# A gated delta-rule attention with a spatial MLP on one core: k's products of the first group as 64x64 tiles, a shorter norm, a new order of operations

## The chip, the cores and the metric

The kernel runs on one core of one Trainium2 chip. The metric is device time in microseconds (us) of one launch. PE is TensorE, DVE is VectorE, ACT is ScalarE, POOL is GpSimd, and SP issues the DMAs. Lower is better.

## The reference, cut to what matters

The input has 4 batches, 8 heads, 768 positions and 48 channels. The attention is a recurrence over positions, and its output feeds a gated MLP with a spatial mixing matrix.

```python
k_n = k / (np.linalg.norm(k, axis=-1, keepdims=True) + 1e-06)
for t in range(S):
    y[:, :, t] = einsum('bhd,bhde->bhe', q[:, :, t], state)
    v_old = einsum('bhde,bhd->bhe', state, k_n[:, :, t])
    state = state + beta_t * einsum('bhd,bhe->bhde', k_n[:, :, t], v[:, :, t] - v_old)
x = y as (batch, 768, 384)
h = np.maximum(x @ w_in, 0.0);  u, v = h[..., :512], h[..., 512:]
v_n = (v - mean(v)) / sqrt(var(v) + 1e-6)
gated = u * (einsum('ts,bsd->btd', w_spatial, v_n) + b_spatial[None, :, None])
out = gated @ w_out
```

## The kernel before, in words

The recurrence is done in chunks of 64 positions. There are 24 steps; a step is one chunk of 2 of the 4 batches, for all heads (16 chains at once), so steps 0 to 11 are one pair of batches and 12 to 23 the other. Four steps form a group, and there are six groups.

For each group, `prep` makes the small triangular matrices that a chunk needs. PE multiplies each chunk of k with itself (`kk`), ACT or DVE copies the products from PSUM to a buffer xt (helper L392), and DVE transposes the diagonal blocks so that each chain sits on a lane of its own (`la`, L576). From the diagonal of the products the norm of k follows (L584 to L591), with it the lane data are scaled (L594 or L598), and the triangular systems are solved on the lanes by forward substitution. Groups 0 and 1 (mode "w") do that on DVE in 16 columns (`lanes16`, L630 to L636, 29 instructions) and are widened to 32 by more matmuls (`widen16`, L706 on); groups 2 to 5 (mode "p") do it on POOL in 32 columns (`lanes`, L615 and L620, 61 instructions). L645 transposes the result back into xt, and `widen` brings each step from 32 to 64 columns.

A step then runs in a fixed chain: `a` on PE (k times the state), DVE subtracts it from v (L782), `b` on PE, ACT copies it (w, L810), `c` on PE, and DVE adds it to the state (S, L823, or L825 in step 0). `qs` and `pu` on PE give the output y, which ACT copies to xs (L841). Two steps make 128 positions of x, which six small DMAs put in order (L858); ACT and DVE split x into a high and a low part (xh L862, xl L863), and then the MLP of these positions can start on PE (`mlp_v`, `mlp_u`; later `mlp_g` and `mlp_o`). A step's chunk of k or q is 256 KB. The weight w_in comes as 64-bit floats in six pieces of 512 KB and is turned into a high and a low part by ten instructions for each piece (L455 to L471) on ACT, DVE and POOL.

Every operation is first added to a plan. `ORDER` is a list written out by hand, two letters for each operation, in which the operations are issued; each engine takes its own in that order and none overtakes another. A pair of letters past the last operation is a filler: a matmul of the mask `mpos` with itself into a free bank, whose result nobody reads. `PICK` chooses the engine where an operation may run on two. The names with L are lines of the profile.

Of the kernel before, what the change touches and what calls it, by code (L numbers as in the profile page):

```python
# [11 lines left out]
ALU = mybir.AluOpType  # L12
# [21 lines left out]
FULL = False  # L34
# [5 lines left out]
    "0407090605000102030J0Y080A0B0KQW0@0*0[QW0D0]0^0_0E0C0L0+0G0|0-0.0/0F0H0I0;1N0<1OQW1Y0N2U0M1P0P2R0:2S2V21221C2XQW2a0Q"  # L40
    "0{1Q0R1R0S0T0U0V1T0W0XQW0}0Z0b0c0d0e0f0g0a0h0i0j0k0l0m0n0oQW0p0q0r0s0tQW112T0u2Y0vQW0wQW0x5K240yQW2W1S0z2Z0O0!QW0#1D"
    "2b375N0$5W3G2c1U5L5Q1k1Z0%2f0~0,QW0&5O2d5T25125MQW38QW0(36100=0>1V1W270?28292D2e1l2h2A2E1E1F1G1I1a2g1H5P2B2C3Q2F132,"
    "3031322N3R0)1K2I2i33142k1m1b2m1c1e1n15171o2t341f2l1dQW162H2G2J3J3S2K1r5R1h2M3539QW2n1q2o2p2q2r2s3F1g19182O5S2j3K3A2u"
    "3L1p5U5V1J3M233H3N8R262P3B1A5Z3O451B3P1i1L1t1X1M2w2x2L2yQW2z2!2#2$3C2%3T2&3~2v2Q2(2)3U2*2+QW2-2.3D5X5Y5a3V3W3X3,403E"
    "QW3a413Y2/2:2;2<2=2>5b4L3Z463b42435c5d4447482?QW4A5e5f5g5h5i5j2@492[2]2^2_4M4N3I8U3eQW4O3i4B3kQW4CQW3h8d3j3d3l3c3f3g"
    "4P4QF74H4S4D4T4FQW5l2{5k5n2|1s5o5p5q2}3m4E4V4R4U4X4W4Y4G4Z4a4c5r8S5s8V2~8T5t515u5v5w8W5x4d5y525z1u1j5!4I3n4b504J1v4m"
    "536U3.3/3:4l5#3o565$4k4f4n4j4i4K4e8a5%8X5&1w1x556V5(5)5*5+5-575.5/3u1y5:1z5;5<5=3v3p5B3q5859546M5A3w5C3;3<6N3=6O5>5D"
    "6T5?3?1!6P3@6Q6R3r6W3[3s3]3^1#3t5@5[5]5^5_5F6j6S5m6X1%5E5{5G5|6k5}6l1$1&3x3y3z3>4o5~1(4h5,3_6Y6f6g1)6m6Z7O4p6a606d6n"
    "61623{6b8Y6c8Z5H6e5I3!5J6o3}1*QW3#631+647W8b7P8c7Q8e4q4g6q7X7R4:4]6566676p1-7S6r68694^4;6t6$4_4<3$1.3%3|8h3&7T6A6s6B"
    "1:6C6D6E6F6G6u7l7U6v6w6&6h6%3(6x1;8f8g4=4{6y4>6!6#6i6)6+6.6-6*6/7m7n1/4r7o4s6H6I6z8i7Y7t7p7h7q1=6J6K7s7V3)8j7r4?4t7u"  # L50
    "7Z6L8l8m4w4|4x7a7b4y7i7j6(8k3*8n8o6:8p8q6;7c7f7d8s4z4!7g9T7e8r9U4u4#4v7v7&8u4}7x4~8v8w8x8y7w7y78798z4@4,9V9q7)7(7A8!"
# [31 lines left out]
PICK = (
    "00000111111100110111011100110010000000100000000000000011001100001100010000000000000000000010010011010010000010000000"
    "00000000000000001000000000100110000010101110100110000000001010010000000000010100101110011011001000000110110100011010"
    "11111100011000100000100010100110100100"
# [181 lines left out]
def delta_rule_gated_mlp(  # L268
# [23 lines left out]
    cst = new("cst", 3)  # L292
# [74 lines left out]
    gd = new("gd", 32)  # L367
# [158 lines left out]
    def prep(g):  # L526
# [56 lines left out]
        bl = bl_[g % 2]  # L583
        P.add("ACT", 0.35, lambda: nc.scalar.activation(out=sq, in_=dg, func=AF.Sqrt, bias=cst[:, 1:2]), rd=[kla, "cst"], wr=["sq"], pr=p0)  # L584
        P.add("ACT", 0.32, lambda: nc.scalar.activation(out=gd, in_=sq, func=AF.Identity, scale=0.5, bias=cst[:, 2:3]), rd=["sq", "cst"], wr=["gd"], pr=p0)
        P.add("DVE", 0.35, lambda: nc.vector.reciprocal(out=t0_, in_=sq), rd=["sq"], wr=["t0"], pr=p0, port=True)
        P.add("DVE", 0.18, lambda: nc.vector.tensor_mul(out=t0_, in0=t0_, in1=dg), rd=[kla], wr=["t0"], pr=p0, port=True)
        P.add("DVE", 0.18, lambda: nc.vector.scalar_tensor_tensor(out=n_l, in0=t0_, scalar=0.5, in1=gd, op0=ALU.mult, op1=ALU.add), rd=["t0", "gd"], wr=["nl"], pr=p0, port=True)
        P.add("DVE", 0.18, lambda: nc.vector.tensor_mul(out=t0_, in0=n_l, in1=n_l), rd=["nl"], wr=["t0"], pr=p0, port=True)
        P.add("DVE", 0.35, lambda: nc.vector.reciprocal(out=t0_, in_=t0_), wr=["t0"], pr=p0, port=True)  # L590
        P.add("DVE", 0.18, lambda: nc.vector.tensor_mul(out=dv, in0=t0_, in1=bl), rd=["t0", ("bl", g % 2)], wr=["sq"], pr=p0, port=True)  # L591
        if mode == "w":
# [530 lines left out]
```

## Time and profile before

| | |
|---|---|
| median of 3 runs | 472.31 us (469.68 to 477.03) |
| the profiled execution: own time | 471.3 us |
| its span, first to last instruction | 469.6 us |
| mean granted TensorE clock | 0.941 of full speed |
| PE busy, matmuls | 427.7 us, 91% of the span |
| DVE, ACT, POOL busy | 248.5, 230.6, 236.4 us |

The time outside the span is 1.7 us. Busy time of PE is the union of matmuls that overlap, so a busy PE is not always PE at its peak. A granted clock of 1.00 is the upper of two levels (2.4 GHz), one of 0.50 the lower (1.2 GHz), and a value between them is a stretch that holds both.

### The profile page before, as it was taken

The numbers are of one execution on the slowest core, as the hardware profiler recorded it, in microseconds if no ns is written. First come the engines' busy times: TensorE is split into PE (matmuls) and PEld (weight loads), VectorE is DVE, ScalarE is ACT, GpSimd is POOL, SyncE is SP. The second block draws the span as 40 slices with busy tenths as digits, with TensorE's granted clock in tenths as the row PEclk, the third lists the DMA queues.
The fourth block names the chain that finished last, engine by engine and source line by source line (L and its number), as shares of the span: only waits on it lengthen the run. The fifth ranks groups of instructions, "written<-read, shape, count | busy, mean of one in ns | idle before, by whom it ended". The sixth has DMA issues, their size and how long they took to land.

```text
span 469.6 us, 21728 instructions
## 1 busy us (share of the span) xinstructions
PE 427.7 (91%) x9736; PEld 379.4 (81%) x9736; DVE 248.5 (53%) x558; ACT 230.6 (49%) x546; POOL 236.4 (50%) x371
## 2 busy tenths in 40 slices
PE   4865986988989999899899999999989999999997
PEld 3654764776777787689899999898888899999996
DVE  4899786375857773686335653425345142251221
ACT  4547634156656677885223553512555570451112
POOL 3274548883468980468973488884213300411220
PEclk9575599798999999899999999999999999999999
DMA  7660314411454455433251023123150000001002
GB/s 273 219 209 25 99 49 125 154 47 57 131 154 139 138 165 175 142 94 103 67 155 44 20 59 109 39 66 116 42 164 3 10 1 0 2 35 50 35 35 84
DMA packets 26109, 42.65 MB, mean 91 GB/s; under 512 B 4512, under 2 KB 14880, under 8 KB 26016
## 3 DMA queue, kind: packets, MB, share of 16 engines
q1 hardware_dynamic: 26016, 41.27, 28.4%
q8 instruction: 76, 1.25, 1.1%
q14 instruction: 17, 0.14, 0.1%
HBM read 35.36 MB, written 4.72 MB: 85 GB/s over the span
## 4 chain that ended last, share of the span: by engine, by line
PE 81%; issue 5%; DVE 3%; ACT 3%; DMA 3%; SPq 2%; POOL 2%; ACTq 0%; DVEq 0%; POOLq 0%
PE ps L524 81%; SPq L411 2%; DMA bn<-in_k_t 2%; ACT xt L392 1%; DMA bn<-in_bun 1%; POOL ut L470 1%; POOL ut L469 1%; ACT w L810 1%; DVE la L576 0%; DVE xt L645 0%; DVE ut L464 0%; DMA xs<-xs 0%; DVE g L464 0%; ACT xs L841 0%; DVE pt L757 0%
## 5 line engine op out<-in xcount | busy, mean ns | idle before, releaser
L524 PE MATMUL ps<-wsph,vf 128*128 128x256 f32 x528 | 107.2, 285 | 0.0
L524 PEld LDWEIGHTS ps<-wsph,vf 128*128 128x128 f32 x528 | 86.6, 190 | 1.1
L620 POOL TENSOR_TENSOR wl<-wl,prod 128x60 f32<-128x60 f32 (+7 forms) x120 | 76.4, 636 | 9.1
L615 POOL TENSOR_TENSOR prod<-wl,la 128x60 f32<-128x60 f32 (+7 forms) x120 | 70.4, 586 | 9.3
L524 PE MATMUL ps<-wspl,vf 128*128 128x256 f32 x264 | 74.6, 283 | 0.0
L524 PEld LDWEIGHTS ps<-wspl,vf 128*128 128x128 f32 x264 | 50.3, 191 | 0.3
L980 DVE TENSOR_TENSOR gt<-ps,bbc 128x512 f32<-128x512 f32 x24 | 16.5, 689 | 52.6 <-PE ps L524 52.5
L524 PE MATMUL ps<-wout_h,g 128*128 128x384 f32 x128 | 35.2, 339 | 0.0
L392 ACT COPY xt<-xt 32x128 f32<-32x128 f32 (+1 forms) x85 | 29.3, 345 | 5.4 <-DVE xt L392 3.6
L524 PE MATMUL ps<-bn 64*64 64x64 f32 (+2 forms) x896 | 19.7, 232 | 9.7 <-DMA bn<-in_k_t 5.9
L983 POOL TENSOR_TENSOR gt<-gt,ut 128x512 f32<-128x512 f32 x11 | 15.1, 1372 | 25.4 <-DVE gt L980 25.3
L524 PEld LDWEIGHTS ps<-bn 64*64 64x64 f32 (+1 forms) x896 | 16.2, 139 | 13.4 <-issue 10.3
L810 ACT COPY w<-ps 128x384 f32<-128x384 f32 x24 | 11.5, 481 | 29.8 <-PE ps L524 29.8
L524 PE MATMUL ps<-mpos 128*128 128x256 f32 x64 | 24.8, 508 | 1.2 <-ACT xs L841 1.0
L985 ACT CAST g<-gt 128x512 fp32r<-128x512 f32 x16 | 9.9, 621 | 31.8 <-DVE gt L983 20.4
L524 PE MATMUL ps<-ke 64*64 64x64 f32 (+2 forms) x768 | 18.4, 254 | 6.7 <-ACT wl L642 3.3
L985 ACT CAST xt<-gt 128x512 fp32r<-128x512 f32 x8 | 5.0, 620 | 39.5 <-POOL gt L983 22.9
L524 PEld LDWEIGHTS ps<-ke 64*64 64x64 f32 (+1 forms) x768 | 15.6, 158 | 10.2 <-issue 4.0
L524 PEld LDWEIGHTS ps<-wout_h,g 128*128 128x128 f32 x128 | 22.9, 188 | 0.3
L757 DVE TENSOR_TENSOR pt<-ps,mpos 128x512 f32<-128x512 f32 (+1 forms) x27 | 16.6, 625 | 11.6 <-PE ps L524 11.3
L887 ACT ACTIVATE vr<-ps 128x512 f32<-128x512 f32 x22 | 13.1, 595 | 18.5 <-PE ps L524 18.3
L739 POOL TENSOR_TENSOR bn<-bn,nn 128x384 f32<-128x384 f32 x14 | 11.9, 854 | 20.0 <-DVE ps L633 5.1
(206 smaller groups left out, 1068.2 us busy)
## 6 DMA issues: line engine op xcount, KB each, us to landing
bn<-in_bun SPq DMA_DIRECT2D x46, 256.0 KB, 3.1
bn<-in_bun SPq DMA_DIRECT2D x48, 192.0 KB, 3.4
ke<-in_k_t SPq DMA_DIRECT2D x22, 256.0 KB, 3.0
out<-ob SPq DMA_DIRECT2D x24, 192.0 KB, 2.0
vf<-in_w_in SPq DMA_DIRECT2D x6, 512.0 KB, 6.1
g<-in_w_sp SPq DMA_DIRECT2D x3, 768.0 KB, 5.3
g<-in_w_out SPq DMA_DIRECT2D x4, 384.0 KB, 4.2
xs<-xs SPq DMA_DIRECT2D x66, 16.0 KB, 2.5
```

The costliest lines, as they stand in the source:

```text
L392: (nc.scalar.copy if e == "ACT" else ENG[e].tensor_copy)(out=out_, in_=in_)
L411: return P.add("SP", 0.39 if k.get("kb") else 0.57, lambda: nc.sync.dma_start(out=out_() if callable(out_) else out_, in_=in_() if callabl ...
L524: nc.tensor.matmul(o, l, r, start=start, stop=stop)
L615: P.add("POOL", cost, lambda: nc.gpsimd.tensor_tensor(out=pt if j else dst, in0=w3[:, :n, j : j + 1].broadcast_to([128, n, m]), in1=la3[:, ...
L620: P.add("POOL", cost, lambda: nc.gpsimd.tensor_tensor(out=dst, in0=dst, in1=pt, op=ALU.add), rd=["prod"], wr=[kw], pr=p0 + 2)
L739: P.add("", {"DVE": 0.56, "POOL": 0.83}, fn=lambda e: ENG[e].tensor_tensor(out=v, in0=v, in1=n.unsqueeze(3).broadcast_to([128, 2, 4, HD]), ...
L757: nc.vector.tensor_tensor(out=pt.rearrange("p (d a c) -> p d a c", d=2, a=2)[:, d], in0=v.rearrange("p d (a c) -> p d a c", a=2), in1=mpos ...
L810: P.add("ACT", 0.48, lambda: nc.scalar.copy(out=v3(w, 192), in_=v3(pc, 512)[:, :, 0:192]), rd=["pc"], wr=[("w", s % 2)], pr=pr)
L887: P.add("ACT", 0.69, lambda: nc.scalar.activation(out=raw_(r), in_=bank(h.unit), func=AF.Relu, accum_out=st[:, j : j + 1]), rd=[("pv", i)] ...
L980: P.add("DVE", 0.69, lambda: nc.vector.tensor_tensor(out=gt(), in0=v3(bank(h.unit), 256), in1=bbc[0][:, th * 256 : th * 256 + 256].unsquee ...
L983: P.add("", both(512), fn=lambda e: ENG[e].tensor_mul(out=gt_[t.unit], in0=gt_[t.unit], in1=u_(uh)[:, half * 512 : half * 512 + 512]), rd= ...
L985: P.add("ACT", 0.6, lambda: nc.scalar.copy(out=gv(gg)[0][:, hs], in_=gt_[t.unit]), rd=[kk], wr=[("gh", b, th, half)], pr=q)
```

## The change

There are three parts. First, `FULL` makes `prep` of group 0 issue the same 16 products of 64x64 for each chunk as the other groups do (32 smaller ones before), and the four copies that put the lower blocks in place (`za`, 32 partitions by 512) now run for group 0 too. Second, the norm is worked out another way. Third, `ORDER` and `PICK` are new: 34 fillers before, one after, and 2376 operations in place of 2372.

```diff
-FULL = False
+FULL = True
-    cst = new("cst", 3)
+    cst = new("cst", 2)
-    gd = new("gd", 32)
+    gd, n2 = new("gd", 32), new("n2", 32)
-        for i, x in enumerate((0.0, 1e-30, EPS)):
+        for i, x in enumerate((0.0, 1e-36)):
-        ACT  sq = activation(dg, Sqrt, bias=1e-30)
-        ACT  gd = activation(sq, Identity, scale=0.5, bias=EPS)
-        DVE  t0 = reciprocal(sq)
-        DVE  t0 = t0 * dg
-        DVE  nl = 0.5 * t0 + gd
-        DVE  t0 = nl * nl
-        DVE  t0 = reciprocal(t0)
-        DVE  dv = t0 * bl
+        ACT  sq = activation(dg, Sqrt, scale=4e-12, bias=1e-36)
+        DVE  n2 = (sq + EPS * EPS) + dg
+        DVE  t0 = reciprocal(n2)
+        DVE  dv = t0 * bl
+        ACT  gd = activation(n2, Sqrt, scale=0.25, bias=1e-36)
+        DVE  t0 = reciprocal(gd)
+        DVE  t0 = t0 * n2
+        DVE  nl = 0.25 * t0 + gd
```

The lines of the norm are shortened to engine, operation and operands; `dv` scales the lanes, and `nl` scales v later.

What the two orders say at their heads, read off the letters (k0 is the chunk of k of step 0, w0 a piece of w_in; the lists of the engines are shown one by one):

```
SP before:  k3 k0 w1 w0 k1 k2 w4 w5 ...
SP after:   w0 w1 k0 k2 w4 k1 k3 q1 w3 ...
DVE before: 5 of w1, 4 of w0 | la(0) | L460 L462 of w4, recip, L464 of w4,
            3 products, recip, L467 of w4, dv, scale | 29 lanes + nn | mask(0) | L645(0)
DVE after:  7 of w0 and w1, L467 L469 of w1, L467 of w0, 4 of w4, mask(1) | la(0) |
            L460 of w3, n2, recip, dv, scale | 29 lanes | recip, t0, nl | L645(0)
ACT after:  the four copies out of PSUM of group 0, then two of its za, then the weights' L455 of w3, then sq
POOL after: two za of group 0, L470 of w1, L470 of w4, ...
```

Here recip, dv, scale and the products are the instructions of the norm, and mask(s) is L757 of step s, which needs q of that step. The last of the six DMAs that order the first positions of x stands in SP's list behind the load of the position-major k (n) of step 3 before (that load waits for `c` of step 1), and the last two behind the load of n of step 4 after (it waits for `c` of step 2). From L645 of group 0 to the state S of step 1 DVE has 66 instructions before and 74 after; the 74 hold the whole norm of group 2 and its scaling.

From L645 of group 0 to xl of the first positions, DVE has 91 instructions in its list before and 90 after. The scaling of group 2's lanes (L598), which releases POOL's first `lanes`, is DVE's 138th instruction before and its 119th after.

## Rows read from the trace of the kernel before

**Rows 1.** The page's busy time and share of the span of each engine.

```profile
PE 427.7 (91%) x9736; PEld 379.4 (81%) x9736; DVE 248.5 (53%) x558; ACT 230.6 (49%) x546; POOL 236.4 (50%) x371
```

**Rows 2.** Stretches: length; busy us of PE, PEld, DVE, ACT, POOL; PE clock; DMA.

```profile
4.00:8.00 4.00, 3.61 (x132) 2.97 (x132) 0.14 (x1) 3.03 (x5) 1.25 (x5) 1.00 0.96 347
36.00:48.00 12.00, 7.08 (x392) 6.29 (x396) 11.16 (x22) 8.48 (x22) 5.64 (x8) 0.50 0.03 8
30.60:81.40 50.80, 38.82 (x1660) 31.09 (x1657) 41.74 (x96) 28.19 (x69) 27.42 (x46) 0.71 0.28 81
83.60:89.30 5.70, 5.70 (x172) 4.86 (x170) 3.58 (x5) 0.43 (x1) 5.15 (x8) 0.50 0.40 105
84.00:200.00 116.00, 108.50 (x3165) 87.58 (x3157) 73.25 (x169) 73.08 (x182) 72.80 (x117) 0.94 0.43 130
200.00:360.00 160.00, 155.17 (x3552) 143.16 (x3550) 78.25 (x174) 72.16 (x177) 101.68 (x165) 1.00 0.27 79
```

**Rows 3.** Stretches, the fillers' passes on PE alone: length; PE busy; clock; DMA.

```profile
60.00:84.00 24.00, 3.93 (x12) 0.99 0.33 95
160.00:180.00 20.00, 1.18 (x4) 1.00 0.52 171
180.00:200.00 20.00, 3.45 (x12) 0.91 0.46 140
sum 470.00, PE 24.76; mean PE 2.75
```

**Rows 4.** PE in order of time: start, duration, what, idle before.

```profile
10.55 0.41 PE L524 MATMUL ps<-ke 64*32 64x64 f32 x26
24.30 0.69 PE L524 MATMUL ps<-ke 64*64 64x64 f32 x32
30.33 1.13 PE L524 MATMUL ps<-ke 64*64 64x64 f32 x32 [3.31 <-ACT wl L642]
85.52 1.01 PE L524 MATMUL ps<-xh,win_h 128*128 128x256 f32 x3
```

**Rows 5.** DVE, and one row of ACT, in order of time.

```profile
13.64 1.95 DVE L576 STREAM_TRANSPOSE la<-xt 128x1024 f32<-128x1024 f32 x1 [1.26 <-ACT xt L392]
15.69 0.35 ACT L584 ACTIVATE sq<-la,cst 128x32 f32<-128x32 f32 x1 [0.98 <-DVE la L576]
17.63 1.18 DVE L589 TENSOR_TENSOR t<-nl 128x32 f32<-128x32 f32 x1
20.41 0.69 DVE L594 TENSOR_TENSOR la<-la,sq 128x512 f32<-128x512 f32 x1
21.21 0.20 DVE L635 SCALAR_TENSOR_TENSOR ps<-ps,la 128x30 f32<-128x30 f32 x1
29.46 0.20 DVE L633 TENSOR_TENSOR ps<-ps,prod 128x30 f32<-128x30 f32 x1
30.60 2.06 DVE L645 STREAM_TRANSPOSE xt<-wl 128x1024 f32<-128x1024 f32 x1
69.44 1.21 DVE L598 SCALAR_TENSOR_TENSOR la<-la,sq 128x1024 f32<-128x1024 f32 x1
80.08 1.32 DVE L863 TENSOR_TENSOR xl<-xs,xh 128x768 fp32r<-128x768 f32 x1
```

**Rows 6.** POOL in order of time.

```profile
17.48 1.28 POOL L469 TENSOR_TENSOR ut<-ut,vf 128x512 f32<-128x512 f32 x1 [12.17 <-ACT vf L466]
```

**Rows 7.** Groups by shape: count, busy us, mean ns, idle before.

```profile
L586 DVE RECIPROCAL t<-sq 128x32 f32<-128x32 f32 x6 | 2.1, 352 | 1.3 <-ACT sq L584 1.3
L392 ACT COPY xt<-ps 128x512 f32<-128x512 f32 x16 | 9.2, 585 | 11.7 <-PE ps L524 11.7
L392 ACT COPY xt<-xt 32x512 f32<-32x512 f32 x13 | 8.0, 615 | 0.2
L392 POOL COPY xt<-xt 32x128 f32<-32x128 f32 x8 | 2.3, 287 | 8.3 <-DVE xt L392 6.4 <-DVE st L903 1.5
```

**Rows 8.** DMA issues of the whole run: count, KB each, median us to landing.

```profile
xs<-xs SPq DMA_DIRECT2D x66, 16.0 KB, 2.5
```

More of the change, by code (lines that the diff above doesn't have):

```diff
@@ new lines @@
+    "0%0&0(0)162g5a2h0]3B5P0*0^0+5S0Y0Z0a5T2i2j5Q2l1b0-2C2M2D1c2k5X5U26291q1r2B170e1s1u182E2F332m3C2G1t2x1w0.3A343U351d36"
+    "2H372o2I2p1J2q2r2w382J2y2!2K3N5Y393D5Z2s3L3O1v3E3P3Q2R1K1e2N1M1f192t1g1x2#1y2$2%2&2(2)2*2u1i1B2v5V3F1C1A1L1j3R1N1P49"
+    "1E1D3S1F1O1l1h5W2n5d5b5e3G5c3X3g8V3T2L2+3J3M2A2O3Y2-2.2/2:2;2<2P5f2Q3Z423a2=3b3i2>2?3h3H3e5g5h3I3f5i3p5j3K2S5o5p1k5r"
+    "2@2[2]2^2_2{2|2}2~2,30431z442T45463c3j4A475k3d4X5s4C4L3o484B4D2U4E4M4F3k8Y3l4N5t5u5v5w5x4P4G4Q4R315y5z5!4J4H4O1Q5#32"
+    "5$4S5%5&5A4T5(1m5)5*5+5-5.1!4U4K4I4V4Y544Z553m3n3q56574b4W5/4a1#4c4d4e4l5:5;3r5<5l8W5=8X4g4h5B4n4pFB5>5?8b5@5[5]1n8Z"
@@ new lines @@
+    "5^5_3s3t2z584f8a596Y4q4o4i3<6Z4k4m3=5C4r3y3>3z6a6Q5D1$8c5{1%5|1&1(1*5}8e5F8d1)3?3!3@6R6S3#3u6T6U6V5G6j4j1+5~1-3[8f3v"
+    "3$3w3%3x5,5m5E5H606X616v6b8g5n6263641.656W6n3_6o3^1/6p6w5I3&6c666d6l4s1:67685J4t1;1<693]6e3{5K6f4u3|3(5L6A6g7S1>1=1?"
+    "1[1@3}6q3~5M4v4w4x3,4y6x6B5N1]6C8l6r6s8k7T413)407U6D1^6k6E6t6u6F6z3*6y3+7p6!6G6H6I3-1_6#7V4z6$6J1{3.7W6h6i6K6&6L6%4!"
+    "4#4>4|1|6(1}1~203/6M7q7a7r8i1,8j6N6*216+22237w6m8h6-6O6P7Z3:6)E,6.6:6;6/7s4$7X7t4?4}7c4~4,504%518m9X6=6<8n9Y4@7Y7l7d"
+    "8o6>9Z7u8p8q4[9a4]4&7b4^7e7f8w8v6?8y4(7m7g9b4{4_7j7h7x8z6@8!8#8$8%8&6[7k53529c7i7v7z7y9f7#7!7$7CIE7n7-7D7o7E6]8(7+8)"
@@ new lines @@
+    "7%7)7*8*9d9u4)4*9g5q4+8+8-8.7&8/8:7.7F7G7H7I8r7(9e7/6^7;7?7>7=9h7:7<9q9j24AZ7J8;8<9i9k9v9w8=8>9l8?8@8[6|9x6_6}Ax9y9#"
+    "9z7K7L9o9m9!6~Ay7@6{9p8]6,7MAz708^718_A!9n7[8{7]A]4-9$8|9&A#727^4.7374A$9%8}8E8~7_7{A^9)9(8s8,9*904/9s7N8F91929t9+A_"
+    "7|7}9/A{7~A%758U9r4=A|A}9:7,7O8G80817P93A&4:9;9=Ab949-8H828IA(9[9>9^9@8J8M8N9<9?9_9]95967R7QAf9798AcA~9.A,A)8O8P8Q8R"
+    "834;76999AAa9B8TA*A-779CA+AgA.AdAhA?A>A/8S9{8L789DAeA:A<B09EA;84B19FB2A=86B49GB3B585B6799H9|9I4<9J879KB7G9GA9}9~9,88"
+    "B8AiA@F2AjAmBCBEGHBHBF9L7A9MF0A38KAJA0A1A4A5A6A7AKALAk7BAn898AA29N9O9P9Q9RF18t9SA88B8u9T8xA9AAAB8CAl9UF3AMANAOACAPAQ"
@@ L85 @@
[L85 to L86 removed]
+    "00001100011110110111011001110110011100000000001100000100001100010100010000000000000000000000000001000100000000000000"
+    "10000000010000000000000000000000000001000000100100001000100000011001000000100100110010000001000111100100011000101011"
+    "000001111101010101100001101000001010001000"
 )
@@ L583, in prep @@
         bl = bl_[g % 2]
[L584 to L590, printed above, removed]
+        P.add("ACT", 0.35, lambda: nc.scalar.activation(out=sq, in_=dg, func=AF.Sqrt, scale=4e-12, bias=cst[:, 1:2]), rd=[kla, "cst"], wr=["sq"], pr=p0)
+        P.add("DVE", 0.18, lambda: nc.vector.scalar_tensor_tensor(out=n2, in0=sq, scalar=EPS * EPS, in1=dg, op0=ALU.add, op1=ALU.add), rd=["sq", kla], wr=["n2"], pr=p0, port=True)
+        P.add("DVE", 0.35, lambda: nc.vector.reciprocal(out=t0_, in_=n2), rd=["n2"], wr=["t0"], pr=p0, port=True)
         P.add("DVE", 0.18, lambda: nc.vector.tensor_mul(out=dv, in0=t0_, in1=bl), rd=["t0", ("bl", g % 2)], wr=["sq"], pr=p0, port=True)
+        P.add("ACT", 0.35, lambda: nc.scalar.activation(out=gd, in_=n2, func=AF.Sqrt, scale=0.25, bias=cst[:, 1:2]), rd=["n2", "cst"], wr=["gd"], pr=p0 + 1)
+        P.add("DVE", 0.35, lambda: nc.vector.reciprocal(out=t0_, in_=gd), rd=["gd"], wr=["t0"], pr=p0 + 1, port=True)
+        P.add("DVE", 0.18, lambda: nc.vector.tensor_mul(out=t0_, in0=t0_, in1=n2), rd=["n2"], wr=["t0"], pr=p0 + 1, port=True)
+        P.add("DVE", 0.18, lambda: nc.vector.scalar_tensor_tensor(out=n_l, in0=t0_, scalar=0.25, in1=gd, op0=ALU.mult, op1=ALU.add), rd=["t0", "gd"], wr=["nl"], pr=p0 + 1, port=True)
         if mode == "w":
```

69 lines of the change are left out of this document (26 added, 43 removed).

## The prediction

> **What bounds the kernel now.** I read the busy times first, then the stretches, then the order of time on PE and DVE. PE is busy 91% of the span [rows 1], but that average covers two regimes. From 84 us on PE is the bound: between 84 and 200 us it is busy 108.5 of 116 us and between 200 and 360 us 155.2 of 160 [rows 2], with matmuls of the MLP that wait for nobody. The first MLP matmul starts at 85.52 [rows 4]. Before that nothing of the kernel's bulk can run, and DVE sets the pace: between 30.6 and 81.4 us it is busy 41.7 of 50.8 us, while PE has time for fillers [rows 2, 3]. So the time is the moment at which the MLP can start, plus PE's work after it, plus PE's waits in that work. A microsecond won ahead of 84 us counts in full as long as PE then finds work; one won on DVE or POOL later counts only where PE waits.
>
> **The change part by part.**
>
> **Arrival of k.** SP's list now puts two pieces of w_in ahead of all chunks of k and a third ahead of the last two. The last product of group 0 starts at 10.55 now [rows 4], behind two pieces; afterwards 512 KB more lie ahead of it. At the 347 GB/s of the first transfers [rows 2] that is 1.5 us, so about 12.1. The product takes 1.1 us at the clock's lower level, where PE will be with almost nothing to do before (the same 32 matmul records took 1.13 at 0.5 and 0.69 at full clock [rows 4]).
>
> **64x64 products.** On PE the smaller number of matmuls costs nothing that counts, because PE waits for transfers there; the cover is the arrival of k, and without it the saving would be some tenths of a us. New are the four copies za. Two are ACT's, 0.62 each, behind four copies out of PSUM of 0.585 [rows 7] and the first step of w4, in one list: from about 12.2 that ends at 15.8. Two are POOL's, in a form that the trace lacks: bounded by 0.6 (ACT's price) and 1.15 (four POOL copies of a quarter of the width, 0.287 each [rows 7]); I take 0.75, nearer ACT's whole copy, and they end near 16.1. In DVE's list mask(1) now stands ahead of la(0): it waits for the 256 KB of q1, 0.8 us behind the last k, and for its product, until about 15. Behind it is only la(0), which waits for za anyway; if q1 came 2 us late, la(0) and all behind it would be late by 1. So la(0) starts at 16.0 (15.0 to 17.0), against 13.64 [rows 5]: 2.4 us later.
>
> **Norm.** From la(0) to the first lane instruction 7.57 us pass now (13.64 to 21.21 [rows 5]). Afterwards: la 1.95, square root 0.35, n2 0.2, reciprocal 0.35, dv 0.2, scale 0.69 [rows 5, 7], together 3.74, and 0.3 for the hand-overs: 4.0. Three instructions fewer are only 0.9 of the 3.5 us gained; the rest is that four steps of w4, one of them stretched, and a product of 1.18 us [rows 5] no longer stand between. Lanes start at 20.0 instead of 21.21. They last 8.4 (21.21 to 29.66 [rows 5]) in both; then reciprocal and two products, 0.75, stand ahead of L645, which starts at 29.2 instead of 30.60: 1.4 us earlier. For groups 2 to 5 the norm saves 0.9 us ahead of POOL's lanes, and from 84 us on that is covered by PE's work.
>
> The product of 1.18 us would be an ordinary 0.2 by its size (L635, of 30 columns in place of 32, takes 0.20 [rows 5]); a POOL instruction on two SBUF operands ran from 17.48 to 18.76 beside it [rows 6]. The Trainium skill, SBUF — State Buffer, section Who interferes with whom, says that a DVE instruction with two SBUF inputs and a reading POOL instruction share a read interface, and that the loser waits for the whole of the other. By that rule the new dv, scale and lanes could each be held once by POOL's four instructions of w1 and w4 that now stand there, and the gain of 1.4 us would go down to about 0; the row agrees with the rule.
>
> **The queue of DVE to the MLP.** From L645(0) to xl DVE has 91 instructions before and 90 after; by the mean durations of their groups that is 43.2 and 43.8 us. It takes 50.8 us now (30.6 to 81.4), with 9.1 idle [rows 2]. What the order changes is where the idle time can fall: the norm and scaling of group 2 and most of group 1's lanes are put ahead of S of step 1 (74 instructions, 32.2 us, in place of 66, 29.9 us), in places where DVE now waits for `c` and for `b`. If no idle time were left, xl would end at 29.2 + 43.8 = 73.0; if all stayed, at 82.1. I take 5 to 6 us of idle, between the two, because PE's part of a step at the lower clock (four times 32 records, 1.1 each instead of 0.7 [rows 4]) stays under DVE's work but the hand-overs to PE, ACT and SP remain. One such wait is new: SP's last two DMAs for x now stand behind a load that waits for `c` of step 2, and xh and xl wait for them. With `c` near 68 us by the sums above, about 1 us for issuing two and 2.5 for landing [rows 8], xl could not start before 72 to 73. That gives xl at 78.5, 3 us earlier (9 earlier to 2 later).
>
> **POOL's lanes of group 2.** They wait for L598 (69.44 [rows 5]), and its place moves from 138th to 119th in DVE's list: by the same sums it comes 8 to 10 us earlier. POOL's lanes of this group then end some 9 us earlier, and with them step 8 becomes ready earlier. PE waits little for that now: 7.5 us of waits in all between 84 and 200 us [rows 2]. I give it 1 us (0 to 4).
>
> **Fillers.** All passes together are 24.8 us of PE, but most lie ahead of 84 us, where PE waits anyway [rows 3]. Their cost counts only between 160 and 200 us, 1.18 + 3.45 = 4.6 us in eight fillers [rows 3], placed beside waits. I take 2 of these 4.6 as gained, since some of the place will be waits. What they gave is the clock: with fillers of 3.9 us in 60 to 84 us the granted clock stays 1.00, and it falls to 0.50 at 83.6 for 5.7 us [rows 2, 3]. Without them it will be 0.50 from early on until the MLP runs, but a start at the lower level is paid now as well (83.6 to 89.3). I count 0 (3 gained to 5 lost).
>
> Sum: 3 + 1 + 2 + 0 = 6 us. Against the execution's own 471.3 us that is 465.3; the median of the runs is 1.0 above that execution, so I forecast **466**.
>
> **The rivals.**
>
> *Half clock (slower).* Between 36 and 48 us PE was busy 7.1 of 12 us at a clock of 0.50; between 60 and 84 us, with 3.9 us of fillers, the clock is at 0.99 [rows 2, 3]. Without fillers any thin place may bring it down. A drop costs half its length in the MLP, 5.7 / 2 = 2.9 us [rows 2]. If the start gains nothing, the 2 us are not gained, and four or five thin places between 84 and 360 us that hold at 1.00 now each drop, the time is 471.3 + 4.5 x 2.9 - 2 = 482. It decides from three such drops on. Against it: from 84 us PE is busy 94%. The Trainium skill, TensorE: Matmul & The Clock Gate, section What's actually happening, calls the lower level the default, which activity releases; that speaks against taking fillers out, and the rows above agree with it. Chance 0.12.
>
> *No change.* The idle time of DVE stays as it is and xl ends at 81 to 82; the new za and the three pieces of w_in eat what the norm saves; the places of the fillers become waits. That is 470 to 473, say 471. For it: only 9 us of DVE's 50.8 are idle at all, and a chain over five engines keeps its hand-overs. Chance 0.28. That the shorter norm doesn't show on the lanes at all, because POOL holds the new instructions as it held the one of 1.18 us, is part of this case.
>
> *More.* DVE loses nearly all its idle time (xl at 74 to 75: 7 us), the eight fillers give their 4.6 in full, and group 2 removes 3 to 4 us of PE's waits around 100 us: 471.3 - 15 = 456. For it: 19 places earlier for L598. Chance 0.22.
>
> **How the numbers follow.** The forecast (462 to 469) has 0.38. The range holds 8 in 10 if it takes in the case "more" to 455 and "no change", and goes to 477 for the milder half of the slower case: 455 to 477. A measurement of this kernel can tell about 2%, 9.4 us, from no change: faster means under 462.9, slower over 481.8. Faster: nearly all of "more" and a fourth of the forecast, 0.31. Slower: the upper half of its case and something for mishaps at the start, 0.09. Within: 0.60.
>
> **What the profile after would show.** la(0) at 15 to 17 us, the first lane instruction 4 us behind it, L645(0) near 29; L598 of group 2 at 59 to 62 instead of 69.4; DVE idle 5 to 6 us from L645(0) to xl; xl ending near 78.5 and the first MLP matmul 2 to 4 us earlier than 85.5; the granted clock at 0.50 from about 12 us until the MLP has run some us; PE's waits between 84 and 200 us not above 7.5. I would be wrong if xl isn't earlier (a wait behind q1, or SP's DMAs behind `c` of step 2), if the clock falls again behind 95 us more than twice, or if PE's waits in the middle grow by as much as the start gains.

## The result, and the profile after

The changed kernel takes 467.03 us (median of 15 runs, 460.38 to 471.21) against 472.68 us of the kernel before on the same chip; the ratio is 0.983, with a 95% interval of 0.980 to 0.987. It is taken from the fast runs of each kernel, so it is not the quotient of those two medians, which is 0.988. Measured a second time the ratio was 0.986 (0.978 to 0.994). So the kernel is 1.2 to 1.7% faster, 6 to 8 us. The forecast was 466 us, 6 us less than before.

The two profiled executions don't show this gain. That of before (471.3 us) lies below the median of its kernel's runs, and that of after (471.2 us) is the longest of its 15; their spans are 469.6 and 469.5 us. Compared row by row, the two traces show what moved, but what the change is worth has to come from many traces and from the ratios. That is the first thing to learn here.

The page of after, busy times, answers to [rows 1]:

```profile
PE 413.8 (88%) x9546; PEld 377.1 (80%) x9546; DVE 249.3 (53%) x573; ACT 233.7 (50%) x555; POOL 226.5 (48%) x349
```

Stretches of after, for [rows 2] (length; busy us of PE, PEld, DVE, ACT, POOL; PE clock; DMA share, GB/s):

```profile
4.00:8.00 4.00, 0.88 (x32) 0.91 (x36) 2.63 (x6) 2.15 (x3) 1.22 (x3) 1.00 1.02 389
30.10:78.90 48.80, 32.59 (x1568) 29.20 (x1568) 40.00 (x100) 27.10 (x66) 32.54 (x46) 0.84 0.35 104
84.00:200.00 116.00, 103.32 (x3020) 86.56 (x3020) 71.23 (x173) 73.99 (x185) 65.38 (x107) 0.94 0.41 127
```

From L644 of group 0 to the end of xl (second row) DVE needs 48.8 us instead of 50.8 and is idle for 8.8 instead of 9.1: the idle time stayed. From 84 to 200 us PE has 5.2 us less work than before (103.3 for 108.5) and 5.2 us more waits (12.7 for 7.5).

PE in order of time, for [rows 4]: the last product of group 0 runs at 11.61, and the first MLP matmul now starts at 84.69 instead of 85.52.

```profile
11.61 1.13 PE L523 MATMUL ps<-ke 64*64 64x64 f32 x32 [0.29 <-ACT xt L391]
77.97 1.05 PE L523 MATMUL ps<-gi,bbc 16*32 16x16 f32 x64 [2.95 <-ACT gi L724]
84.69 0.97 PE L523 MATMUL ps<-win_h,xh 128*128 128x512 f32 x3
```

The two starts are not of the same product. Before, the first one is of v (xh as the weights, 85.52), and the first of u (w_in as the weights) follows at 87.61; afterwards u comes first, and v follows at 86.46. Ahead of the start PE has about 32 small products more than before (fillers and the halves of group 0 left out).

The row 10.55 of [rows 4] is only the first 26 of the 64 products of its chunk; the rest came behind a stop of PE:

```profile
12.24 0.67 PE L524 MATMUL ps<-ke 64*32 64x32 f32 x38 [1.28 <-issue]
```

"issue" is a wait for which the profile shows no releaser.

DVE in order of time, for [rows 5] (the lines of the code are one lower than before from here on):

```profile
14.84 1.95 DVE L575 STREAM_TRANSPOSE la<-xt 128x1024 f32<-128x1024 f32 x1 [0.39 <-POOL xt L391]
17.84 1.24 DVE L586 TENSOR_TENSOR sq<-t,bl 128x32 f32<-128x32 f32 x1
19.12 1.69 DVE L593 TENSOR_TENSOR la<-la,sq 128x512 f32<-128x512 f32 x1
20.91 0.20 DVE L634 SCALAR_TENSOR_TENSOR ps<-ps,la 128x30 f32<-128x30 f32 x1
30.08 2.06 DVE L644 STREAM_TRANSPOSE xt<-wl 128x1024 f32<-128x1024 f32 x1
58.08 1.23 DVE L597 SCALAR_TENSOR_TENSOR la<-la,sq 128x1024 f32<-128x1024 f32 x1
77.78 1.10 DVE L862 TENSOR_TENSOR xl<-xs,xh 128x768 fp32r<-128x768 f32 x1 [1.64 <-ACT xh L861]
```

POOL in order of time, for [rows 6]: the two copies za, and two products on operands in SBUF.

```profile
13.54 1.26 POOL L391 COPY xt<-xt 32x512 f32<-32x512 f32 x2 [8.27 <-ACT xt L391]
17.76 1.27 POOL L469 TENSOR_TENSOR ut<-ut,win_h 128x512 f32<-128x512 f32 x1 [1.71 <-ACT win_h L467]
18.99 1.27 POOL L470 TENSOR_TENSOR win_l<-ut 128x512 fp32r<-128x512 f32 x1
```

Put beside the DVE rows, these show the hold: dv (32 columns) starts at 17.84 and ends at 19.08, with POOL's first product (19.03); the scaling starts at 19.12 and ends at 20.81, which is the end of POOL's second product (20.26) plus most of its own 0.69 [rows 5]. Without POOL they would take 0.2 and 0.7: 2.0 us are lost.

The wait of 2.95 us on PE is a chain over SP, the DMA, ACT and PE. SP's queue, then ACT:

```profile
70.47 2.01 SPq L410 DMA_DIRECT2D bn<-in_bun  x2
72.53 1.15 SPq L410 DMA_DIRECT2D xs<-xs  x2
76.91 0.83 ACT L861 CAST xh<-xs 128x768 fp32r<-128x768 f32 x1 [3.29 <-DMA xs<-xs]
77.65 0.27 ACT L724 ACTIVATE gi<-ps 128x128 f32<-128x128 f32 x1
```

The last DMAs for x stand behind a load, xh waits for them, gi stands behind xh in ACT's list, and PE waits for gi.

### The profile page after: what moved, and what is told of

The parts are those of the page before. It is cut to its first block, busy times and chain, and to the rows that moved or that the text cites. A ratio compares the mean times of both kernels' runs of the same rounds, so it can differ in the third digit from the quotient of the medians.

```text
span 469.5 us, 21334 instructions
## 1 busy us (share of the span) xinstructions
PE 413.8 (88%) x9546; PEld 377.1 (80%) x9546; DVE 249.3 (53%) x573; ACT 233.7 (50%) x555; POOL 226.5 (48%) x349
## 4 chain that ended last, share of the span: by engine, by line
PE 80%; DVE 6%; issue 5%; ACT 5%; DMA 3%; SPq 1%; POOL 0%; ACTq 0%; POOLq 0%; DVEq 0%
PE ps L523 80%; ACT xt L391 1%; DMA vf<-in_w_in 1%; SPq L410 1%; DVE la L575 1%; DVE ps L632 1%; DMA ke<-in_k_t 1%; DMA xs<-xs 1%; DVE prod L629 1%; DMA bn<-in_bun 1%; ACT vf L465 1%; ACT win_h L467 0%; ACT wspl L391 0%; DVE la L593 0%; ACT w L809 0%
## 5 line engine op out<-in xcount | busy, mean ns | idle before, releaser
L619 POOL TENSOR_TENSOR wl<-wl,prod 128x60 f32<-128x60 f32 (+7 forms) x120 | 72.9, 607 | 9.3
L391 ACT COPY xt<-xt 32x128 f32<-32x128 f32 (+1 forms) x92 | 32.4, 352 | 3.0 <-DVE xt L391 0.9
L523 PE MATMUL ps<-ke 64*64 64x64 f32 x704 | 20.1, 270 | 11.6 <-DMA ke<-in_k_t 3.8
L523 PEld LDWEIGHTS ps<-ke 64*64 64x64 f32 x704 | 16.9, 176 | 14.2 <-ACT wspl L391 4.7
L822 DVE TENSOR_TENSOR s<-s,ps 112x384 f32<-112x384 f32 x20 | 11.0, 550 | 32.5 <-PE ps L523 32.2
L523 PE MATMUL ps<-bn 64*64 64x64 f32 x832 | 20.8, 250 | 7.1 <-DMA bn<-in_k_t 7.1
L984 ACT CAST g<-gt 128x512 fp32r<-128x512 f32 x16 | 9.8, 619 | 31.2 <-DVE gt L982 25.2
L523 PEld LDWEIGHTS ps<-bn 64*64 64x64 f32 x832 | 17.8, 161 | 9.4 <-DVE ut L461 7.1
L920 POOL TENSOR_TENSOR vf<-vr,vf 128x512 fp32r<-128x512 f32 x5 | 6.6, 1329 | 37.1 <-ACT vf L919 37.1
L391 ACT COPY xt<-ps 128x512 f32<-128x512 f32 (+1 forms) x32 | 14.9, 478 | 17.8 <-PE ps L523 17.8
L1000 ACT COPY ob<-ps 128x384 f32<-128x384 f32 x24 | 11.2, 478 | 22.7 <-PE ps L523 21.1
```

The costliest lines, as they stand in the source:

```text
L391: (nc.scalar.copy if e == "ACT" else ENG[e].tensor_copy)(out=out_, in_=in_)
L523: nc.tensor.matmul(o, l, r, start=start, stop=stop)
L619: P.add("POOL", cost, lambda: nc.gpsimd.tensor_tensor(out=dst, in0=dst, in1=pt, op=ALU.add), rd=["prod"], wr=[kw], pr=p0 + 2)
L822: P.add("DVE", 0.55, lambda: nc.vector.tensor_tensor(out=sv, in0=sv, in1=pv, op=ALU.add), rd=["pc"], wr=["S"], pr=pr)
L920: P.add("", both(512), fn=lambda e: ENG[e].tensor_sub(out=full_(f)[:, DH : 2 * DH], in0=raw_(r), in1=full_(f)[:, 0:DH]), rd=[kk, ("vh", i) ...
L984: P.add("ACT", 0.6, lambda: nc.scalar.copy(out=gv(gg)[0][:, hs], in_=gt_[t.unit]), rd=[kk], wr=[("gh", b, th, half)], pr=q)
```

## The experiments

All ratios are to the kernel before on the same chip, with the 95% interval in brackets; each edited kernel ran 6 or 12 times and left one trace.

**The changed kernel again**, for its spread and a second trace.

> The changed kernel itself, once more, as the common reference of this set. Expected 464 to 468 us beside 472 to 473 of the kernel before, and a trace in which xl of the first positions ends between 77 and 80 us. If the granted clock is again 1.00 up to 60 us although PE has little to do, the clock at the start is not set by the fillers alone; if it is 0.50 from about 12 us on, the first trace was an exception.

Measured: 0.986 (0.978 to 0.994). Its granted clock is 0.50 from 30 to 60 us, where the first trace has 1.00, with the same PE work (20.7 and 20.3 of 30 us); the first MLP matmul starts at 84.67 against 84.69. So between these two executions the clock ahead of the MLP did not move its start.

**Fillers out of the kernel before.**

```diff
-    34 fillers in ORDER
```

> The kernel before with its 34 fillers taken out of the list and nothing else changed. My theory (the order of DVE's queue at the start carries the gain): 1 to 3 us faster than before (ratio 0.994 to 0.998), first MLP matmul within 1 us of 85.5. Rival (the missing fillers are the gain): 5 us or more faster, as fast as the changed kernel. Rival (fillers hold the clock): slower by 3 us or more, with a clock of 0.50 between 60 and 84 us.

Measured: 1.000 (0.996 to 1.003). PE without its fillers is not faster, and not slower for want of them. The one trace misses the expected MLP start: 91.20, in an execution 4.5 us above its kernel's median. Its granted clock from 60 to 84 us is 0.64, so the clock is lower, as the third rival has it, but the kernel is not slower.

**The old norm in the new order.**

```diff
-        ACT sq, DVE n2, t0, dv, ACT gd, DVE t0, t0, nl
+        ACT sq, gd, DVE t0, t0, nl, t0, t0, dv
```

> The changed kernel with the old norm (eight instructions, all ahead of the scaling of the lanes), at the places of the new one; the transposes of the norms of groups 1 and 2 come earlier. My theory: the lanes of group 0 start 0.8 to 1 us later and the kernel is 0 to 2 us slower than the changed one. Rival (the norm is the gain): 4 us or more slower, near the kernel before.

Measured: 0.994 (0.990 to 0.999). The lanes of group 0 start 0.5 us later, but the scaling of group 2 comes at 61.77 instead of 59.02 and 58.08, S of step 1 (L822) at 65.83 instead of 63.09 and 62.49, the first MLP matmul at 85.95. By the ratios that is some 4 us slower than the changed kernel on the same chip (0.986), by the medians 2.8, between the theory and the rival, and the two intervals overlap. It fits that in this order DVE's extra instructions of three groups add up.

**Group 2 later in the new order.**

```diff
 DVE: ... L644 of group 1
+     n2, t0, dv, L597 of group 2
      S of step 2
```

> The changed kernel with the norm and scaling of group 2's lanes (four DVE instructions) and POOL's first lanes of that group moved behind group 1's transposed result, ahead of the state of step 2, about where the kernel before has them. POOL's lanes of group 2 should start 11 to 13 us later and the state of step 1 about 2 us earlier. My theory: PE has MLP work by then, so the kernel changes by less than 3 us either way. Rival (the early start of group 2's lanes is what carries the gain): slower by 5 us or more, with PE waiting around 100 to 115 us.

Measured: 0.988 (0.983 to 0.994), with L597 14 to 15 us later and the MLP started at 84.62:

```profile
73.25 1.22 DVE L597 SCALAR_TENSOR_TENSOR la<-la,sq 128x1024 f32<-128x1024 f32 x1
```

The theory held, but S of step 1 did not come earlier (63.32). No difference from the changed kernel can be told: that POOL's lanes of group 2 are early buys little or nothing.

**The last DMAs for x earlier.**

```diff
 SP:
+     xs, xs
      load n(4)
-     xs, xs
 ACT:
-     xh
      gi
+     xh
```

> The changed kernel with SP's last two DMAs for x put ahead of the load that waits for c of step 2, and with the reciprocal-root step gi of u's first rows (ACT) put ahead of xh. Theory: in the changed kernel these two DMAs land at about 77 us, xh waits 3.3 us for them on ACT with gi behind it, and PE waits 2.95 us for gi just ahead of the MLP. Taken away, gi runs at about 75, the product f16 no longer waits, xh at about 74.5, xl ends near 77.5 instead of 78.9, the first MLP matmul is 1 to 3 us earlier (82 to 83.5 instead of 84.7), and the time is 1 to 3 us under the changed kernel's: a ratio of 0.978 to 0.983 against the kernel before. Rival: the first MLP matmul waits for xl, which stands behind S of step 2 and the bias products in DVE's queue and not behind the DMAs; then PE's wait of 2.95 us moves to another place, the MLP starts at 84.3 or later and the ratio stays at 0.984 to 0.988.

Measured: 0.988 (0.982 to 0.994). xl starts at 75.94 instead of 77.78, as expected. But the product behind gi ended only 0.5 us earlier (78.52 for 79.02), since it now stopped in its middle:

```profile
75.92 0.49 PE L523 MATMUL ps<-gi,bbc 16*32 16x16 f32 x19 [0.53 <-ACT gi L724]
77.69 0.83 PE L523 MATMUL ps<-gi,bbc 16*32 16x16 f32 x45 [1.28 <-issue]
84.42 0.96 PE L523 MATMUL ps<-win_h,xh 128*128 128x512 f32 x3
```

The rival's outcome held: the 2.95 us moved. But it was not xl that the MLP waited for, since xl ends at 77.31; behind the stop PE's products of a step follow to 84.4.

**POOL's products away from dv and the scaling.**

```diff
 ACT:
-     cast of w4
      rounding of w0
      copy of dv (L603)
+     cast of w4
```

> The changed kernel with ACT's cast of w4 that releases POOL's two-operand instructions put behind the copy of dv onto the diagonal, so that no POOL instruction on two operands in SBUF runs beside dv and the scaling of group 0. Theory that POOL's instruction holds DVE's: dv takes 0.2 to 0.25 us instead of 1.24, the scaling 0.7 instead of 1.69, the first lane instruction starts at about 18.9 instead of 20.7 to 20.9, L644 of group 0 at about 28.0 instead of 29.9 to 30.1. Of these 2 us the MLP start gets 0.5 to 1.5 us; ratio 0.981 to 0.985. Rival: the two are long for another reason (their own operands); then both durations stay and so does everything behind. Second rival: they get short, but the chain over PE and ACT ahead of 84 us eats the 2 us; then L644 is earlier and the ratio is 0.984 to 0.988 all the same.

Measured: 0.981 (0.974 to 0.988). DVE, then POOL:

```profile
17.81 0.19 DVE L586 TENSOR_TENSOR sq<-t,bl 128x32 f32<-128x32 f32 x1
18.04 0.69 DVE L593 TENSOR_TENSOR la<-la,sq 128x512 f32<-128x512 f32 x1
18.84 0.20 DVE L634 SCALAR_TENSOR_TENSOR ps<-ps,la 128x30 f32<-128x30 f32 x1
...
18.85 1.27 POOL L469 TENSOR_TENSOR ut<-ut,win_h 128x512 f32<-128x512 f32 x1 [2.83 <-ACT win_h L467]
```

The same instructions on the same operands take 0.19 and 0.69 instead of 1.24 and 1.69. The hold is shown. L644 of group 0 comes at 28.38 (1.5 to 1.7 earlier), the MLP starts at 83.17 (1.5 earlier).

**Both edits.**

> The changed kernel with both edits: SP's two DMAs for x and gi earlier, and POOL's two-operand instructions behind dv and the scaling. If the two gains add up, the first MLP matmul starts 2 to 4 us earlier than in the changed kernel (81 to 83 us) and the ratio is 0.975 to 0.981; if the MLP start hangs on another wait, the ratio stays at 0.984 to 0.988.

Measured: 0.984 (0.980 to 0.989), MLP start at 82.36. The MLP start is 2.3 us earlier than in the changed kernel, but the ratio can't be told from the changed kernel's, nor can that of the edit before. A gain of either over the changed kernel isn't shown.

**The new norm in the kernel before**, twice: with the three instructions for the norm itself behind the lanes, and where nn stands.

```diff
-        ACT sq, gd, DVE t0, t0, nl, t0, t0, dv
+        ACT sq, DVE n2, t0, dv, ACT gd, DVE t0, t0, nl
```

> The kernel before, in its own order and with its own tiles and fillers, with the new norm alone (six DVE instructions in place of seven on the path, the three for the norm itself behind the lanes of groups 0 and 1). Theory that the norm is the larger part of the change's gain: scaling of group 0 0.5 to 1 us earlier than 20.41, S of step 1 1 to 3 us earlier, ratio 0.989 to 0.994. Rival: the new order and the earlier places are what gains, and the norm shows only together with them; then ratio 0.997 to 1.000.

Measured: 1.006 (1.002 to 1.010). POOL's product with nn (L739) waited for nn until 31.2 us, and its other products behind it then fell on DVE's steps of w_in, DVE first, then POOL:

```profile
34.88 1.38 DVE L462 TENSOR_SCALAR ut<-ut 128x512 uint32<-128x512 uint32 x1
37.97 1.38 DVE L467 TENSOR_SCALAR ut<-ut 128x512 uint32<-128x512 uint32 x1
...
34.51 1.46 POOL L470 TENSOR_TENSOR ut<-ut,win_h 128x512 f32<-128x512 f32 x1
37.35 1.72 POOL L470 TENSOR_TENSOR ut<-ut,win_h 128x512 f32<-128x512 f32 x1
```

Steps that take 0.43 elsewhere took 1.38. So this kernel doesn't price the norm, and the next one was made.

> The kernel before in its own order with the new norm alone; the three instructions for the norm itself stand where the old kernel has its transpose nn, among the lanes, so that POOL's product with nn is not held back as it was when they stood behind the lanes. Theory: the norm's two or three fewer instructions on DVE ahead of the lanes are worth what they measure, 0.9 us a group, and not 4 us; lanes of group 0 start 0.3 to 1.3 us earlier than with the old norm at the same arrival of k, and the ratio is 0.996 to 1.000. Rival: the norm is the change's main term, as the kernel with the old norm in the new order suggested; then 0.989 to 0.994.

Measured: 1.000 (0.996 to 1.004). The first theory held: in the old order the shorter norm, as it falls there, is worth nothing that can be measured. But here too POOL held dv (1.25 us from 18.93, beside a product of POOL from 18.68), and from la(0) to the lanes 7.20 us pass instead of 7.57. What the norm would give in the old order without the hold was not tried.

**Half tiles of group 0 in the new order.**

```diff
-FULL = True
+FULL = False
-    4 copies za of group 0
```

> The changed kernel with group 0's products of k as half tiles again (64x32 and the like, as in the kernel before) and without the four copies za, all else in the new order. Theory that the four copies hold the first transpose back: la(0) starts at 14.0 to 14.3 instead of 14.7 to 15.0, everything of group 0 behind it 0.5 to 0.8 us earlier, MLP start 0 to 0.7 us earlier, ratio 0.981 to 0.986 (nothing that can be told from the changed kernel). Rival: the half tiles, twice as many matmuls for each chunk at a start with a low clock, take PE longer than the copies take ACT and POOL; then la(0) starts at 15 or later and the ratio is 0.986 to 0.990.

Measured: 0.987 (0.981 to 0.992). la(0) is 2.3 us late, but for a reason that neither side named: the stream of 64 small matmuls for the last chunk stopped in its middle, as it does in the kernel before (1.28 us) and in that with the new norm in place (1.24). The whole tiles have 32 matmuls there, and in eight traces with them no such stop falls on that chunk.

```profile
14.62 0.64 PE L523 MATMUL ps<-ke 64*32 64x32 f32 x36 [2.45 <-issue]
17.10 1.89 DVE L575 STREAM_TRANSPOSE la<-xt 128x1024 f32<-128x1024 f32 x1
86.18 1.57 PE L523 MATMUL ps<-win_h,xh 128*128 128x512 f32 x3
```

Of the 2.3 us at la(0), 1.5 are left at the MLP start (86.18) and none can be told in the ratio.

**k first in the new order.**

```diff
 SP:
+     k0, k2
      w0, w1
-     k0, k2
+     k1, k3
      w4
-     k1, k3
```

> The changed kernel with k's four chunks of group 0 put on SP's queue ahead of the pieces of w_in (two ahead of the first, two ahead of the third), all else the same. Theory that k's arrival sets la(0): 0.5 MB less lies ahead of the last chunk, at 380 to 390 GB/s 1.3 us, so the last product of group 0 comes 1 to 1.4 us earlier, la(0) at 13.4 to 14.0 instead of 14.7 to 15.0, lanes 0.5 to 1.2 us earlier, ratio 0.981 to 0.985. Rival: the transfers' rate falls where k's chunks are first, as in two traces of the old order (137 to 168 GB/s between 4 and 6 us, where the new order moves 390); then the second chunk is late, la(0) stays at 14.5 to 15 and the pieces of w_in come later, the ratio is 0.985 to 0.992.

Measured: 0.989 (0.984 to 0.994). The rival's ratio held, and the rate from 4 to 8 us fell to 302 GB/s from 389. But la(0) came 3.6 us later, not earlier, and not for want of k:

```profile
4.00:8.00 4.00, 3.09 (x65) 2.25 (x64) 0.44 (x1) 0.00 (x0) 1.22 (x3) 1.00 0.87 302
...
8.58 0.66 ACT L454 ACTIVATE ut<-vf 128x512 f32<-128x512 f32 x1 [5.89 <-DMA vf<-in_w_in]
...
14.54 1.54 ACT L391 COPY xt<-ps 128x512 f32<-128x512 f32 x3
...
18.39 1.95 DVE L575 STREAM_TRANSPOSE la<-xt 128x1024 f32<-128x1024 f32 x1 [0.39 <-POOL xt L391]
```

PE's first product of k starts at 3.59 instead of 7.12. ACT's copies of the products, however, stand in its list behind steps of w_in, and the first of these now starts at 8.58 instead of 5.01. So the copies (L391), which begin at 10.99 in the changed kernel, come 3.6 us later, and la(0) with them. The edit shows that in this order w_in sets la(0) through ACT's list; what an early k would give with the copies ahead of these steps was not tried.

**w_in first in the kernel before.**

```diff
 SP:
+     w1, w0
      k3, k0
-     w1, w0
+     w4
      k1, k2
-     w4
```

> The kernel before with SP's first loads in the changed kernel's manner: the first two pieces of w_in ahead of k's first two chunks, the third ahead of the last two; all else as before. Theory that a part of the change's gain is a steadier start, which the one trace of before doesn't show because it was a lucky one: the rate stays at 380 to 400 GB/s from 4 to 8 us, the last two products of group 0 wait less, la(0) at 13.5 to 15, the MLP starts at 84.5 to 87.5 (85.5, 87.5, 91.2 and 91.2 in four traces of the old order) and the ratio is 0.985 to 0.994. Rival: the start is no nearer to the end than the other parts that were tried alone, and the gain needs the whole new order; then the MLP starts at 87 to 91 and the ratio is 0.996 to 1.003.

Measured: 1.007 (1.002 to 1.011). The rate was steady at 402 GB/s from 4 to 8 us and the MLP started at 86.87, but there is no gain. So nothing is left of the theory that a steadier start is a part of it, as far as the old order goes.

## Why the prediction was right, point by point

**No part alone carries it.** In the old order, taking the fillers out, the new norm and the new order of loads give 1.000, 1.000 and 1.007: no gain. The whole tiles alone in the old order were not tried. In the new order, going back on one part leaves 0.987 to 0.989, and 0.994 for the norm. So the gain needs the new order, and by the point values more than half of it needs the shorter norm inside that order (0.994 with the old one, against 0.983 and 0.986; its interval is clear of the first of these and overlaps the second). That this is because DVE is queued up ahead of S of step 1 there fits the later S of step 1 in that run, and was not tried apart.

**Where the time went** is read from all 14 traces. The parts of each span: L645 (L644) of group 0, the first MLP matmul, the rest from there to the end, and of the rest what the lower clock cost, as the sum of (1 - granted clock) x length over stretches of 3 us. That last column is an estimate: it takes PE as busy, and bound by its clock, throughout.

| kernel | L645 | MLP start | rest | lost to the clock in the rest |
|---|---|---|---|---|
| before | 30.60 | 85.52 | 384.1 | 6.0 |
| before, no fillers | 31.34 | 91.20 | 384.8 | 13.2 |
| before, new norm | 31.65 | 91.17 | 386.5 | 7.2 |
| before, new norm in place | 30.94 | 87.51 | 386.5 | 8.9 |
| before, w_in first | 31.29 | 86.87 | 385.7 | 3.4 |
| after | 30.08 | 84.69 | 384.8 | 8.6 |
| after again | 29.87 | 84.67 | 383.8 | 5.9 |
| after, old norm | 30.56 | 85.95 | 387.3 | 6.8 |
| after, group 2 late | 30.04 | 84.62 | 380.3 | 2.6 |
| after, x earlier | 30.19 | 84.42 | 383.9 | 6.0 |
| after, POOL moved | 28.38 | 83.17 | 381.1 | 4.5 |
| after, both | 28.57 | 82.36 | 379.9 | 3.4 |
| after, half tiles | 32.37 | 86.18 | 376.7 | 0.7 |
| after, k first | 33.62 | 87.41 | 380.7 | 3.4 |

In the mean the MLP starts at 88.5 in the old order and at 84.8 in the new one, 3.6 us earlier. The two traces at 91.2 are of executions 4 us above their kernels' medians; without them it is 1.8. The rest is 385.5 against 382.1 us. These means mix the two kernels with edited ones, of which two start 1.5 and 2.3 us earlier than the changed kernel itself.

**The term MLP start (3 us).** Right in direction; its size is not settled. The traces of the two kernels themselves show 0.8 us (84.69 and 84.67 against 85.52), the means 1.8 to 3.6. By its steps: *la(0)* was to start at 16.0 and started at 14.67 to 15.00 in the kernels with the new loads and tiles, at or under the range's lower end. k's last product came at 11.61 instead of 12.1. ACT copied three of the four banks from 10.99 on, beside the last products, where the sum had all four copies behind them; so POOL's za, 0.63 each and near the lower bound, were done at 14.80 instead of 16.1.

```profile
10.99 1.54 ACT L391 COPY xt<-ps 128x512 f32<-128x512 f32 x3
```

The prediction's "some tenths of a us" for the smaller number of matmuls left out the stop of 1.28 us in row 12.24, which the 64x64 products don't have. *Norm to lanes* was to take 4.0 and took 6.1 (14.84 to 20.91): the difference is POOL's hold of dv and the scaling, 2.0 us. The hold that the prediction set beside its sum, and gave to the case of no change, is what came: in the run without the overlap dv and the scaling take 0.19 and 0.69. The Trainium skill, SBUF — State Buffer, section Who interferes with whom, says that a DVE instruction with two inputs in SBUF and a reading POOL instruction exclude each other, and that run agrees. The two errors partly cancel: lanes at 20.91 instead of 20.0, L644 at 30.08 instead of 29.2, 0.5 us gained where 1.4 were forecast. *The queue of DVE*: xl was to end at 78.5 and ended at 78.9; but of DVE's 9.1 idle us only 0.3 went, not 3 to 4. Its work up to xl is 40.0 us, 41.7 before. The wait named as new, SP's DMAs behind a load, is there with 3.3 us on ACT, but it is not the last: removed, the MLP starts 0.3 us earlier.

**The term group 2 (1 us).** L597 came at 58.08, just under the forecast 59 to 62. Worth: 0 to 0.5%, not told apart from nothing.

**The term fillers (2 us).** Their work went: PE has 5.2 us less between 84 and 200. It became waits, 5.2 us more of them; those of the kind "issue" alone grew by 5.6, from 3.4 to 9.0 (engine and line, what for, us, times, longest):

```profile
PE ps L523 <- issue: 9.0, 7, 2.6
```

This is the condition of the rival *no change* ("the places of the fillers become waits"), and it held. "PE's waits not above 7.5" was wrong, and they grew by more than the start gained in these two traces, which the prediction's last sentence names as a sign of being wrong.

**The term clock (0).** This step failed, to the good side. The prediction paid a start at the lower clock in both kernels. In all five traces of the old order about 3 to 7 of the MLP's first 8 us run at 0.50; in the new order, in nine traces, 1.6 at most. By (1 - clock) x length over the first 8 us that is 2.4, 2.4, 1.4, 3.4 and 3.2 us against 0 in six, 0.2, 0.7 and 0.8: 2.4 us in the mean. The stretches around the MLP start of the kernel before with the norm in place (start at 87.51):

```profile
83.51:85.51 2.00, 0.39 (x44) 0.28 (x39) 0.38 (x2) 0.80 (x2) 1.76 (x4) 1.00 0.35 128
85.51:87.51 2.00, 1.58 (x122) 1.38 (x122) 0.65 (x2) 0.83 (x2) 1.76 (x4) 1.00 0.21 43
87.51:89.51 2.00, 1.55 (x12) 1.46 (x7) 1.90 (x4) 0.00 (x0) 1.76 (x4) 0.50 0.40 134
89.51:91.51 2.00, 2.00 (x44) 1.35 (x46) 0.13 (x1) 0.00 (x0) 1.84 (x3) 0.50 0.14 32
91.51:93.51 2.00, 2.00 (x51) 1.67 (x36) 0.00 (x0) 0.28 (x1) 1.76 (x4) 0.50 0.64 179
```

And those of after (start at 84.69):

```profile
74.69:76.69 2.00, 0.33 (x34) 0.22 (x26) 1.34 (x3) 0.00 (x0) 1.76 (x4) 0.50 0.01 1
78.69:80.69 2.00, 2.00 (x90) 1.96 (x82) 0.76 (x4) 0.00 (x0) 1.84 (x3) 0.50 0.04 8
80.69:82.69 2.00, 1.40 (x60) 1.24 (x60) 0.18 (x1) 0.48 (x1) 1.76 (x4) 0.50 0.00 0
82.69:84.69 2.00, 1.97 (x88) 1.70 (x80) 0.73 (x2) 1.22 (x3) 1.79 (x3) 0.75 0.37 104
84.69:86.69 2.00, 2.00 (x38) 1.47 (x39) 0.00 (x0) 0.62 (x2) 1.82 (x3) 1.00 0.07 18
```

In three of the five traces of the old order PE has a thin spot just ahead of the MLP (0.39, 0.39 and 0.55 of 2 us), and the clock falls when the dense work has begun. Most of that spot is a stop of PE in the middle of 64 small products; in the kernel before:

```profile
82.71 0.35 PE L524 MATMUL ps<-wspl,bbc 32*16 32x16 f32 x26 [1.24 <-issue]
```

In the new order the thin spot lies 8 us ahead, the low level with it, small products of a step run behind it, and the clock is back at 1.00 before or with the first MLP matmul. The other two traces of the old order have no such spot: without fillers the clock had stood at 0.50 for over 16 us, and with the new norm it fell although PE was busy 1.65 and 1.62 us of the two stretches of 2 us before. So all 14 traces show the low clock behind the MLP start in the old order and next to none of it in the new one; why is not shown. Nor do the traces of the two kernels themselves show the gain over the whole rest: 6.0 us are lost to the clock before, 8.6 and 5.9 after.

The fillers of the old order did not secure the clock either: from 60 to 84 us it is 0.99 in the kernel before [rows 3], but 0.71, 0.78 and 0.91 in the other three traces with fillers, and 0.64 without. Taking them out cost nothing here: the ratio without them is 1.000. The rule that the prediction weighed against it (the Trainium skill, TensorE: Matmul & The Clock Gate, section What's actually happening) had the lower level as the default, which activity releases.

**The rival *half clock*.** Its time didn't come, but its condition did in one trace: behind 95 us the clock falls four times in the first trace of the changed kernel (twice in that of before), which is over the "more than twice" that the prediction named as a sign of being wrong. In the other eight traces of the new order it falls none to three times.

**Sum.** 3 + 1 + 2 + 0 = 6 was forecast; by the traces it is 0.8 to 3.6 for the MLP start and 2.4 for the clock behind it, with group 2 and the fillers near nothing. So the time came out with one term in the place of another, and that it came out so near is luck: two of the signs of being wrong showed in the first trace. Shown are the hold by POOL, what the fillers, the norm and the loads are worth alone in the old order, and the low clock behind the MLP's start. That the two shares make up the ratio is worked out from means over traces of kernels that also differ in other things, and was not tried by a run that moves PE's thin spot alone.

## What to carry to other kernels

When two traces agree to 0.1 us and the ratios say 1.5%, look at where in its kernel's spread each profiled execution lies, and read milestones over all traces at hand. A chain's gain is worth what the next dense stage gets: ask not only when it starts, but at what clock. A load put earlier wins nothing when the next engine has other work ahead of it in its list: k came 3.5 us earlier, and la(0) 3.6 us later. Before costing a short instruction on two operands in SBUF, look for POOL's instructions at that moment: here 0.2 us became 1.24, and moving one ACT cast took it away.

## What the runs showed that was not expected

**Much of the scatter goes with the clock.** From the MLP start to the end the traces of the new order differ by 10.6 us (376.7 to 387.3); less the clock's share in the last column of the table, eight of the nine lie between 376.0 and 377.9 us (the old norm's is 380.5). In the old order it doesn't come out so: 371.6 to 382.3. In after there are four drops behind the MLP start, of 1.7 to 3.4 us each; in the kernel with half tiles there is none but 0.7 us at the start itself.

**PE stops in streams of small matmuls** without a releaser in the profile: 2.45 us among 64 matmuls of 32 columns, 1.28 us in the product of 64 behind gi, and 9.0 us in all from 84 to 200 us of after against 3.4 before. They go with a DMA queue that the page of after lists as that of the instructions (packets, MB, share):

```profile
q8 instruction: 75, 1.23, 1.1%
```

Each packet has 16 KB. Of the 142 such stops of over 0.8 us in the 14 traces, 140 end 1.0 to 1.7 us after a packet of this queue has landed, where 11% of PE's matmuls start that long after one. So PE most likely waits for instructions there; no run changed their number or place for this alone. These stops also stand by the drops of the clock: of the 19 drops behind 95 us in the new order's nine traces, 18 begin during such a stop or within 1.5 us of its end, though not every stop has one (the longest in after, 2.61 us to 197.48, has none). Since fillers, tiles and order all move the places where PE's instructions run out, this is a rival to the account of the thin spot above, and it was not tried.
